# One attention burst a step, a second inverse on GpSimdE and the first network's weights on ScalarE's queue

## The chip, the cores and the metric

The kernel runs on one core of a Trainium2 chip. The metric is the device time of one execution in microseconds (us). TensorE does matmuls into the eight PSUM banks; VectorE, ScalarE and GpSimdE do the elementwise work (GpSimdE has no part in PSUM here); SyncE (SP) issues the DMAs. The engines run their own instruction lists in order and meet through semaphores.

## The reference

For 4 batches and 8 heads of 768 positions with 48 values a head, a delta rule carries a 48 x 48 state from position to position; its output, 3072 tokens of 384 values, goes through two networks (384 to 2048 to 384), the first with a rational function, the second with a squared relu:

```
for t in range(S):
    y[:, :, t] = q_t @ state
    v_old = state^T @ k_t                      # k_t normalised
    state = state + beta_t * outer(k_t, v_t - v_old)
h = x @ w_in; P = a0 + a1*h + a2*h**2 + a3*h**3; Q = 1 + |b0|*|h| + |b1|*h**2
x2 = (P / (Q + 1e-6)) @ w_out
h = x2 @ w2_in; r = max(h, 0); out = (r * r) @ w2_out
```

## The kernel before

**Attention.** The positions are cut into 12 chunks of 64, so there are 48 pieces (chunk, batch), each with all 8 heads, in 6 groups of 8. For each piece the 64 steps of the rule become matmuls with a 64 x 64 triangular inverse `T`. A group first needs its inverses: the products of the keys (`gram`, line 439) go through DRAM (`gs`) into `Gb`, a forward substitution fills `Tt`, and two matmul stages (`m1` line 619, `m2` line 633) join two 32 x 32 blocks to one of 64. Groups 0 and 1 substitute 15 steps of 16 x 16 blocks on VectorE (line 493) and join them with further 32 x 32 matmuls on TensorE (`ma`, `mb`, `mc`, lines 569 to 596) into 32 x 32 inverses. Groups 2 to 5 do 31 steps of 32 x 32 on GpSimdE (lines 502 to 508) and need no `ma`, `mb`, `mc`; the result goes through DRAM (`td`, `nd`). All groups use one `Gb`, one `Tt` and one `tmp`.

**One step.** A piece takes one step. `first` (line 729) makes `H` (keys times queries and state, `kv`) of piece k and, from group 1 on, `U` (`T` times the corrected values, `tv`) of piece k-1 beside it. `middle` (line 748) copies and masks `H` and corrects the values. `rest` (line 767) copies `U`, makes the output `Y` (`c3`, line 777) and then the state's increment `dS` (`ku`), with, in groups 1 to 3, the `gram` of piece n+16 beside it. `products` (line 711) interleaves generators two matmuls at a time; fp32 matmuls show up as two records each.

**PSUM.** Banks 0 to 2 accumulate the networks' second products (`acc`). Banks 3 to 5 are the pool `h`, for the first products; a bank of it is held from `mm1` until line 948 has read it for the last time. Banks 6 and 7 are the pool `att`; after group 0 attention has these two alone.

**The networks.** For each of 6 blocks of 512 tokens and each of 16 slices of the hidden layer there is a unit: `mm1` (line 912, 9 matmuls 128x512), the function (`rational`, line 931, eleven operations on ScalarE, VectorE and GpSimdE), `mm2_1` (line 953, 6 matmuls). The 96 units of the first network interleave with the attention of the groups to come; the second network's 96 units follow. A weight slice of 768 KB (fp64 bits) is loaded by SP (`dma`, line 330), turned into fp32 halves by ScalarE and VectorE (lines 863 to 870), and its remainder is made by GpSimdE (line 880). Ten of the 16 slices of the first network pass through two `raw` buffers.

**The order.** No order is written by hand. `Plan` lists every piece of work with an engine, an estimated duration, a due time and the tiles that it reads and writes; `play` simulates the engines greedily and the best of eight rounds is written out as each engine's list. Estimates and due times so set the order, and a wait is paid on the chip where an estimate is wrong. `PL.fill` adds matmuls on a constant where the plan sees TensorE idle near the start.

Of the kernel before, what the change touches and what calls it, by code (L numbers as in the profile page):

```python
# [19 lines left out]
C = 64  # L20
# [16 lines left out]
PREF = 1.5  # L37

# [204 lines left out]
def kernel(ctx, tc, kT, kS, qT, kn, vn, beta, par_in, w1, w2, outT):  # L243
# [55 lines left out]
    PL.fill = (T0 - 64, T0 + 20, lambda: nc.tensor.matmul(banks[2][:, 0:N // 2], ones[:, 0:128], ones, start=True, stop=True), 0.16, FILL)  # L299
# [6 lines left out]
    Gb, Tt = (x[:, 0:1024].rearrange("p (a b) -> p a b", b=32) for x in (Gbf, Ttf))  # L306
# [3 lines left out]
    tmp = at.tile([128, 256], F32, name="tmp")  # L310
# [14 lines left out]
    nd = [dram.tile([128, 32, 32] if g < 2 else [2, 32, 32, 32], F32, name=f"nd{g}") for g in range(NG)]  # L325
# [121 lines left out]
    def gstore(n, due):  # L447
        either(0.37, 0.36, lambda: (slot["Gs", n], ps(("G", n), [128, NP, C])), r=[("G", n)], w=[("Gs", n)], due=due,
            alloc=(("Gs",), ("Gs", n)), free=[("G", n)])
        dma(128, gs[n // 8][:, n % 8], lambda: slot["Gs", n], r=[("Gs", n)], w=[("gs", n)], due=due, free=[("Gs", n)])  # L450

    def attention(g):
        d0, d1 = inv_due(g)
        if g:
# [7 lines left out]
            for i in range(2):  # L462
                for j in range(2):
                    o = 64 * j + 32 * i
                    dma(128, Gb[o:o + 32], gv[j, i, :, :, 32 * i:32 * i + 32], lat=3.8, iss=0.6,
                        r=[("gs", 8 * g + ss) for ss in range(8)], w=[("Gb", o)], due=d0 - 3)
        else:
            add("DVE", 2.1, lambda: V.transpose(Gb, Dg.rearrange("r s p c -> r c (s p)")), lock=1,
                r=[("Dg", n) for n in range(8)] , w=[("Gb", o) for o in (0, 32, 64, 96)] + [("TT", 0)], due=d0)
        GB = [("Gb", o) for o in (0, 32, 64, 96)]  # L470
# [4 lines left out]
        add("POOL", 1.0, lambda: P_.memset(Tt, 0.0), w=["Tt"], due=d0)  # L475
# [13 lines left out]
        add("DVE", 0.25, lambda: V.tensor_copy(Tt.rearrange("p a b -> p (a b)")[:, 0:1024:33], nbr), r=["nbr"], w=["Tt"], due=d0, lock=1)  # L489
        for s in range(15 if g < 2 else 0):  # L490
# [7 lines left out]
            add("DVE", 0.42 + 4.0e-3 * a * b, st16, r=GB, w=["Tt", "tmp"], due=d1, lock=1)  # L498
        for s in range(31 if g > 1 else 0):
# [9 lines left out]
            for st in (st1, st2):  # L509
                add("POOL", 0.17 + 2.3e-3 * a * b, st, r=GB, w=["Tt", "tmp"], due=d1, lock=1)  # L510
# [5 lines left out]
        elif g == 1:  # L516
            for o in range(0, 128, 32):
                c0 = o % 64
                src = gs[g].rearrange("r s p c -> r (s p) c")[o + 16:o + 32, :, c0:c0 + 16]
                dma(32, Nb[o + 16:o + 32, :, :, 0:16].rearrange("r s p c -> r (s p) c"), src, lat=2.5, iss=0.6,  # L520
                    r=[("gs", 8 * g + ss) for ss in range(8)], w=[("N", o)], due=d1)


        if g:
            gv = gs[g].rearrange("r s p c -> r (s p) c")
            for o in (32, 96):
                if g == 1:
                    dma(128, TN[o:o + 32].rearrange("r s p c -> r (s p) c"), gv[o:o + 32, :, 0:32], lat=3.0, iss=0.6,
                        r=[("gs", 8 * g + ss) for ss in range(8)], w=[("TN", hf, o) for hf in range(2)], due=d1)
                for hf in range(2) if g > 1 else ():  # L530
# [3 lines left out]
        if g < 2:  # L534
            add("DVE", 2.0, lambda: V.transpose(Gb.rearrange("r q c -> r c q"), Tt.rearrange("p a b -> p b a")), r=["Tt"], w=GB, due=d1, lock=1)
            add("DVE", 2.0, lambda: V.transpose(DN.rearrange("r s p c -> r c (s p)"), Tt), r=["Tt"], w=["DN"], due=d1 + 1, lock=1)
        else:
            dma(512, td[g], Tt, r=["Tt"], w=[("td", g)], due=d1, lat=2.0)
            add("ACT", 2.05, lambda: A_.copy(Gb, Tt.rearrange("p a b -> p b a")), r=["Tt"], w=GB, due=d1)
# [10 lines left out]
        for i in (1, 0) if g > 1 else ():  # L550
            for j in range(2):
                o = 64 * j + 32 * i
                dma(128, TTv[o:o + 32, :, 32 * i:32 * i + 32], tdv[i, j], r=[("td", g)], w=[("TTx", g % 2, i, j)],
                    due=d1 + 2, lat=3.4, iss=0.6, after=[PL.last[wT[0]]] if wT[0] in PL.last else [])
        if g > 1:
            for j in range(2):
                dma(128, nd[g][j], Gb[64 * j:64 * j + 32], r=GB, w=[("nd", g, j)], due=d1 + 2)
                for hf in range(2):
                    x = 64 * j + 32 * hf
                    dma(64, TN[x:x + 32, 4 * hf:4 * hf + 4].rearrange("r s p c -> r (s p) c"), nd[g][j][16 * hf:16 * hf + 16].rearrange("q r c -> r q c"),  # L560
                        r=[("nd", g, j)], w=[("TN", hf, x)], due=d1 + 3, lat=3.2, iss=0.6)
                dma(64, TTv[64 * j:64 * j + 32, 16:32, 32:64], tdv[1, j][:, 16:32], r=[("td", g)], w=[("T", g % 2, 1, 64 * j)], due=d1 + 2, lat=3.2, iss=0.6)
# [3 lines left out]
        for hf in range(2 if g < 2 else 0):  # L566
# [47 lines left out]
        four = g > 1  # L614
        hs = range(2) if four else range(1)
        for hf in range(1 if four else 2):
# [33 lines left out]
            td_ = [("TD", g, hf, o) for o in range(0, 128, 32)] if g < 2 else []  # L650
# [78 lines left out]
        def first(k, k2, due):  # L729
# [374 lines left out]
```

## Time and profile before

| | |
|---|---|
| median of 3 runs | 1109.71 us (1107.1 to 1110.93) |
| the profiled execution | 1110.19 us, span of its instructions 1108.5 us |
| mean granted TensorE clock | 0.963 of 2.4 GHz |
| TensorE busy | 1057.7 us (95%) |
| VectorE, ScalarE, GpSimdE busy | 703.4, 647.6, 401.2 us |

The profiled execution lies 0.48 us above the median. Busy times are those of instructions in the profile; matmuls are pipelined, so their single durations overlap and a stretch is better measured from start to start.

### The profile page before, as it was taken

What the parts mean: (1) busy time and instruction counts of PE and PEld (TensorE: products, weight loads), DVE (VectorE), ACT (ScalarE), POOL (GpSimd) and SP (SyncE); (2) the same over time, 40 slices, a digit from 0 to 9 for tenths busy, and PEclk for the clock granted to TensorE, in tenths of its full rate; (3) what the DMA queues carried; (4) which work ended last, traced back from release to release, by engine and by line L of the source; (5) the groups of instructions that cost most, each with busy time, mean ns of one, the idle gap of its engine ahead of it and who ended that gap; (6) DMA issues with size and microseconds to landing.
All of it is one profiled execution on the core that took longest, in us unless ns stands there. A gap on an engine that the chain in (4) does not pass through costs nothing.

```text
span 1108.5 us, 24471 instructions
## 1 busy us (share of the span) xinstructions
PE 1057.7 (95%) x10014; PEld 752.1 (68%) x10014; DVE 703.4 (63%) x1124; ACT 647.6 (58%) x1173; POOL 401.2 (36%) x540
## 2 busy tenths in 40 slices
PE   6588999799989999999999899999999999999998
PEld 5576665466656666666666555688888888888887
DVE  5658889888658768766777599994334343333432
ACT  5264788676767777677778588754333242333422
POOL 6104589569628844972233143551000000000000
PEclk7677899999999999999999999999999999999999
DMA  7455326741650174034010220720001010000000
GB/s 235 120 144 166 75 90 190 166 128 31 144 116 34 50 161 110 5 103 83 29 28 12 90 85 30 252 89 29 29 0 57 1 51 8 1 29 1 29 1 29
DMA packets 120544, 84.01 MB, mean 76 GB/s; under 512 B 88048, under 2 KB 105584, under 8 KB 120432
## 3 DMA queue, kind: packets, MB, share of 16 engines
q1 hardware_dynamic: 120432, 82.44, 26.8%
q8 instruction: 79, 1.29, 0.5%
q14 instruction: 33, 0.27, 0.1%
HBM read 63.41 MB, written 17.83 MB: 73 GB/s over the span
## 4 chain that ended last, share of the span: by engine, by line
PE 84%; DVE 6%; POOL 3%; issue 3%; DMA 3%; ACT 1%; SPq 1%; DVEq 0%; ACTq 0%; POOLq 0%
PE bank L921 33%; PE bank L957 19%; PE bank L983 6%; PE bank L981 6%; PE bank L982 6%; PE bank L721 6%; PE bank L780 2%; PE bank L640 1%; POOL Tt L508 1%; DMA X<-in_qT_dram 1%; PE bank L626 1%; POOL tmp L504 1%; POOL mem L941 1%; PE bank L585 1%; DVE tmp L495 1%
## 5 line engine op out<-in xcount | busy, mean ns | idle before, releaser
L921 PE MATMUL bank<-xh,A 128*128 128x512 f32 x1152 | 360.6, 394 | 1.1 <-POOL A L880 1.1
L957 PE MATMUL bank<-mem,B 128*128 128x512 f32 x576 | 278.7, 615 | 0.7 <-DVE mem L948 0.7
L921 PE MATMUL bank<-xl,A 128*128 128x512 f32 x576 | 256.5, 445 | 6.0 <-DVE mem L948 5.2
L921 PEld LDWEIGHTS bank<-xh,A 128*128 128x128 f32 x1152 | 218.2, 190 | 63.4 <-issue 15.1
L941 POOL TENSOR_TENSOR mem<-mem 128x512 f32<-128x512 f32 x96 | 129.1, 1344 | 202.4 <-ACT mem L939 201.9
L957 PEld LDWEIGHTS bank<-mem,B 128*128 128x128 f32 x576 | 104.3, 192 | 97.5 <-issue 84.3
L969 DVE SCALAR_TENSOR_TENSOR mem<-bank,mem 128x512 f32<-128x512 f32 x96 | 66.3, 690 | 151.3 <-ACT mem L968 151.1
L968 ACT ACTIVATE mem<-bank 128x512 f32<-128x512 f32 x96 | 57.4, 598 | 152.9 <-PE bank L921 151.0
L921 PEld LDWEIGHTS bank<-xl,A 128*128 128x128 f32 x576 | 109.1, 189 | 45.9 <-issue 15.5
L983 PE MATMUL bank<-gh,C 128*128 128x512 f32 x288 | 113.7, 395 | 0.0
L981 PE MATMUL bank<-gl,C 128*128 128x512 f32 x288 | 113.5, 394 | 0.0
L982 PE MATMUL bank<-gh,C 128*128 128x512 f32 x288 | 112.0, 389 | 0.0
L972 DVE TENSOR_TENSOR gl<-mem,gh 128x512 fp32r<-128x512 f32 x96 | 71.5, 745 | 63.3 <-ACT gh L971 63.2
L946 DVE SCALAR_TENSOR_TENSOR mem<-mem,par,bank 128x512 f32<-128x512 f32 x96 | 71.3, 743 | 53.4 <-ACT bank L945 53.2
L971 ACT CAST gh<-mem 128x512 fp32r<-128x512 f32 x96 | 59.6, 621 | 74.8 <-DVE mem L969 62.0
L944 ACT ACTIVATE mem<-mem,par 128x512 f32<-128x512 f32 x96 | 69.3, 722 | 36.0 <-POOL mem L941 35.2
L942 DVE TENSOR_TENSOR mem<-bank,mem 128x512 f32<-128x512 f32 x96 | 65.8, 685 | 31.6 <-ACT mem L347 30.8
L938 ACT ACTIVATE mem<-bank 128x512 f32<-128x512 f32 x96 | 57.1, 595 | 46.1 <-PE bank L921 41.2
L939 ACT ACTIVATE mem<-mem,par 128x512 f32<-128x512 f32 x96 | 78.1, 814 | 2.3
L508 POOL TENSOR_TENSOR Tt<-Tt,tmp 128x31 f32<-128x31 f32 (+15 forms) x124 | 72.4, 584 | 8.2
L943 DVE SCALAR_TENSOR_TENSOR mem<-mem,par,bank 128x512 f32<-128x512 f32 x96 | 71.6, 745 | 3.9 <-ACT mem L938 1.4
L347 ACT COPY X<-bank 64x192 f32<-64x192 f32 (+1 forms) x184 | 62.0, 338 | 18.3 <-DVE vn L764 9.7
(124 smaller groups left out, 1546.4 us busy)
## 6 DMA issues: line engine op xcount, KB each, us to landing
raw<-in_w_dram SPq DMA_DIRECT2D x18, 768.0 KB, 5.5
B<-in_w_dram SPq DMA_DIRECT2D x10, 768.0 KB, 4.8
kTg<-in_kS_dram SPq DMA_DIRECT2D x40, 128.0 KB, 3.3
gs<-Gs SPq DMA_DIRECT2D x40, 128.0 KB, 2.5
kTc<-in_kT_dram SPq DMA_DIRECT2D x40, 128.0 KB, 2.5
X<-in_qT_dram SPq DMA_DIRECT2D x96, 48.0 KB, 2.9
kn<-in_kn_dram SPq DMA_DIRECT2D x12, 384.0 KB, 4.1
vn<-in_vn_dram SPq DMA_DIRECT2D x12, 384.0 KB, 3.6
```

The source lines that it names most:

```text
L508: P_.tensor_tensor(Tt[:, 0:a, s + 1:32], Tt[:, 0:a, s + 1:32], tv, op=ALU.subtract)
L921: M.matmul(h, a, b, start=(k == 0 and m == 0), stop=(k == NK - 1 and m == 2))
L939: add("ACT", 0.83, lambda: A_.activation(b(), a(), AF.Identity, bias=s(4), scale=s(5)), r=[ak, "par"], w=[bk], due=due + 3.3, alloc=(("b", ...
L941: add("POOL", 1.32, lambda: P_.tensor_tensor(b(), b(), a(), op=ALU.mult), r=[ak], w=[bk], due=due + 4.2, lock=1)
L943: add("DVE", 0.75, lambda: V.scalar_tensor_tensor(c(), c(), s(1), h(), op0=ALU.add, op1=ALU.mult), r=[hk, "par"], w=[ck], due=due + 6.3)
L944: add("ACT", 0.72, lambda: A_.activation(a(), b(), AF.Ln, bias=s(6)), r=[bk, "par6"], w=[ak], due=due + 6)
L946: add("DVE", 0.75, lambda: V.scalar_tensor_tensor(c(), c(), s(0), h(), op0=ALU.add, op1=ALU.mult), r=[hk, "par"], w=[ck], due=due + 8)
L957: M.matmul(acc[d], Bw[j][:, 128 * d:128 * d + 128], slot[gk], start=(j == 0), stop=(j == NJ - 1))
L972: add("DVE", 0.72, lambda: V.tensor_tensor(gl(), b(), gh(), op=ALU.subtract), r=[bk, gk, "late"], w=[lk], due=due + 5, lock=1, alloc=(("gl ...
L981: M.matmul(acc[d], wh, gl, start=(j == 0), stop=False)
L982: M.matmul(acc[d], wl, gh, start=False, stop=False)
L983: M.matmul(acc[d], wh, gh, start=False, stop=(j == NJ - 1))
```

## The change

Three things change together, and the plan makes a new order from all of them.

1. In groups 1 to 5 one `burst` a step takes the place of `first`, `c3` and `dS`: at step t it runs `c3` of piece t-2 and then, interleaved in one call of `products`, `kv` of piece t, `tv` of piece t-1, `ku` of piece t-2 and the `gram` of piece t-1+16. A group has 10 bursts. A burst allocates its banks together, up to three, from `att` and `h`; the `gram` lies in the rest of `U`'s bank. Copies between bursts are unchanged.
2. Group 1's inverse goes the way of groups 2 to 5: 31 steps on GpSimdE, `td` and `nd`, no `ma`, `mb`, `mc`, joined `m1` and `m2`. Even and odd groups have their own `Gb`, `Tt` and `tmp`. Its due times become 30 and T0 + 35. Latencies of `td`, `TTx`, `nd` and `TN` in the plan are raised.
3. The first network's 16 weight loads are issued by ScalarE, planned from 16 us on, 5.5 us apart; two tasks on the plan's pseudo engine LAND stand for their landing. The fill matmuls stop once `mm2_1` has begun. A scratch of the program for dynamic DMAs is cut to 1024 bytes.

```
-    tmp = at.tile([128, 256], F32, name="tmp")
+    tmps = [at.tile([128, 256], F32, name=f"tmp{i}") for i in range(2)]
...
         if g == 1:
-            return T0 - 10, T0 + 20
+            return 30, T0 + IV1
...
+        Gb, Tt, tmp = Gbs[q], Tts[q], tmps[q]
...
-        for s in range(15 if g < 2 else 0):
+        for s in range(0 if g else 15):
...
-        for s in range(31 if g > 1 else 0):
+        for s in range(31 if g else 0):
...
-        for hf in range(2 if g < 2 else 0):
+        for hf in range(0 if g else 2):
...
-        four = g > 1
+        four = g > 0
...
+        def burst(t, due):
+            r, w, al, fr, dur = [], [], [], [], 0.0
+            k0, k1, k2 = (x if 0 <= x < 8 else None for x in (t, t - 1, t - 2))
+            m = 8 * g + k1 + 16 if k1 is not None and g < NG - 2 else None
+            if k2 is not None:
...
+                w, al, dur = w + [("Y", n), ("dS", n)], al + [(("att", "h"), ("Y", n))], dur + 0.65
+            if k0 is not None:
...
+                w, al = w + [("H", n)], al + [(("att", "h"), ("H", n))]
+            if k1 is not None:
...
+                w, al = w + [("U", n)], al + [(("att", "h"), ("U", n))]
...
+            def go():
+                if k2 is not None:
+                    c3(8 * g + k2)
+                products(*([kv(k0)] if k0 is not None else []), *([tv(k1)] if k1 is not None else []),
+                         *([ku(k2)] if k2 is not None else []), *([gram(m, slot["U", m - 16][:, NP * D:NP * (D + C)].rearrange("r (p c) -> r p c", p=NP))] if m else []))
+            q = max((0.76 if k0 is not None else 0) + (0.36 if k2 is not None else 0), (0.37 if k1 is not None else 0) + (0.44 if m else 0))
+            add("PE", 0.22 + dur + q, go, r=r, w=w, due=due, alloc=al, free=fr)
...
+        for t in range(10 if g else 0):
+            dn = step_due(8 * g + t) if t < 8 else step_due(8 * g + 7) + 3 * (t - 7)
+            burst(t, dn)
+            if t < 8:
+                middle(t, dn + 1)
+            if 0 < t < 9:
+                ucopy(t - 1, dn + 1)
+            if t > 1:
+                result(t - 2, dn)
...
+        if l == 1:
+            add("ACT", 0.3, lambda: A_.dma_start(raw(rk), src[j]), w=[(rk, 0)], due=2 + 4.5 * j, alloc=None if e else (("raw",), rk), nb=WB + WS * j)
+            q = add("LAND", WS - 0.3, lambda: None, r=[(rk, 0)], w=["wq"], due=d0 - 4)
+            add("LAND", 2.5, lambda: None, w=[rk, (rk, 1)], due=d0 - 2, after=[q])
```

## Rows read from the trace of the kernel before

**Rows 1.** The page's first part: busy us (share of the span) xinstructions.
```profile
PE 1057.7 (95%) x10014; PEld 752.1 (68%) x10014; DVE 703.4 (63%) x1124; ACT 647.6 (58%) x1173; POOL 401.2 (36%) x540
```

**Rows 2.** Busy time of each engine in four stretches (granted clock, DMA share, GB/s last).
```profile
40.00:60.00 20.00, 13.23 (x623) 11.98 (x621) 6.70 (x10) 7.69 (x14) 2.43 (x2) 0.50 0.52 123
...
80.00:100.00 20.00, 15.37 (x524) 12.86 (x519) 18.69 (x30) 9.73 (x25) 11.90 (x12) 0.87 0.73 211
...
160.00:200.00 40.00, 38.74 (x510) 23.40 (x508) 36.98 (x59) 30.78 (x61) 37.38 (x52) 1.00 0.58 174
...
400.00:500.00 100.00, 99.44 (x1089) 61.54 (x1089) 73.04 (x125) 72.91 (x135) 63.52 (x97) 1.00 0.39 90
```

**Rows 3.** The chain that ended last, 340 to 400 us: start, us, what.
```profile
345.54 2.58 PE bank L957 x6
348.12 2.06 PE bank L921 x9
...
362.04 2.06 PE bank L921 x9
...
375.00 2.06 PE bank L921 x9
...
382.16 2.07 PE bank L921 x9
```

**Rows 4.** TensorE's timeline through one step with gram, 375 to 390 us.
```profile
377.00 0.26 PE L780 MATMUL bank<-X 112*48 112x64 f32 x1
...
377.58 0.25 PE L721 MATMUL bank<-X,kn 64*48 64x48 f32 x2
...
378.20 1.98 PE L957 MATMUL bank<-mem,B 128*128 128x512 f32 x4
380.12 0.31 PE L721 MATMUL bank<-X,kTc 48*64 48x112 f32 x2
...
381.03 1.13 PE L957 MATMUL bank<-mem,B 128*128 128x512 f32 x2
```

**Rows 5.** The same timeline in group 5, where no gram runs.
```profile
489.11 0.56 PE L721 MATMUL bank<-X,kn 64*48 64x48 f32 x16
489.61 0.50 PE L921 MATMUL bank<-xl,A 128*128 128x512 f32 x1
```

**Rows 6.** TensorE's timeline through the first network's first block.
```profile
103.50 0.80 PE L921 MATMUL bank<-xl,A 128*128 128x512 f32 x1
...
128.50 0.53 PE L585 MATMUL bank<-mem,DN 32*32 32x32 f32 x40 [1.76 <-issue]
...
201.36 0.67 PE L721 MATMUL bank<-vn,TT 64*64 64x48 f32 x16 [1.98 <-ACT X L347]
...
213.93 0.88 PE L921 MATMUL bank<-xh,A 128*128 128x512 f32 x2 [0.61 <-POOL A L880]
...
224.21 0.79 PE L921 MATMUL bank<-xl,A 128*128 128x512 f32 x1
```

**Rows 7.** VectorE's timeline before the first block: group 1's transposes.
```profile
82.33 2.07 DVE L535 STREAM_TRANSPOSE Gb<-Tt 128x1024 f32<-128x1024 f32 x1
...
87.52 1.95 DVE L536 STREAM_TRANSPOSE DN<-Tt 128x1024 f32<-128x1024 f32 x1
```

**Rows 8.** GpSimdE's substitutions of groups 2 to 5: busy us, mean ns.
```profile
L508 POOL TENSOR_TENSOR Tt<-Tt,tmp 128x31 f32<-128x31 f32 (+15 forms) x124 | 72.4, 584 | 8.2
...
L504 POOL TENSOR_TENSOR tmp<-Gb,Tt 128x31 f32<-128x31 f32 (+15 forms) x124 | 65.2, 526 | 9.7 <-DVE Tt L489 0.2
```

**Rows 9.** The tile raw up to 240 us: ns min/median/max.
```profile
L332 SPq DMA_DIRECT2D raw<-in_w_dram x12: 327/394/3859, 50.0 to 225.4; - x12
...
L865 DVE SCALAR_TENSOR_TENSOR raw<-raw x10: 959/1231/1978, 89.9 to 208.3; 128x768 uint32<-128x768 uint32 x10
```

**Rows 10.** What SP's queue waited for up to 200 us: us, times, longest.
```profile
SPq L332 <- POOL A L880: 11.6, 3, 5.2
```

**Rows 11.** The full timeline inside the step of rows 3, VectorE.
```profile
373.48 0.68 DVE L948 SCALAR_TENSOR_TENSOR mem<-bank,mem 128x512 f32<-128x512 f32 x1
```

More of the change, by code (lines that the diff above doesn't have):

```diff
@@ L298 @@
     nc.gpsimd.memset(ones, 1.0)
-    PL.fill = (T0 - 64, T0 + 20, lambda: nc.tensor.matmul(banks[2][:, 0:N // 2], ones[:, 0:128], ones, start=True, stop=True), 0.16, FILL)
+    begun = []
+    PL.fill = (T0 - 64, T0 + 20, lambda: begun or nc.tensor.matmul(banks[2][:, 0:N // 2], ones[:, 0:128], ones, start=True, stop=True), 0.16, FILL)
     X = [at.tile([128, 2, NP, 112], F32, name=f"X{b}") for b in range(B)]
@@ L324 @@
     td = [dram.tile([128, 32, 32], F32, name=f"td{g}") for g in range(NG)]
-    nd = [dram.tile([128, 32, 32] if g < 2 else [2, 32, 32, 32], F32, name=f"nd{g}") for g in range(NG)]
+    nd = [dram.tile([2, 32, 32, 32], F32, name=f"nd{g}") for g in range(NG)]
     y1 = [dram.tile([DM, N], F32, name=f"y1_{i}") for i in range(NT)]
@@ L526, in attention @@
             for o in (32, 96):
[L527 to L530, printed above, removed]
+                for hf in range(2):
                     x = o - 32 * hf
@@ L549, in attention @@
         wT = [("TT", g % 2)]
-        for i in (1, 0) if g > 1 else ():
+        for i in (1, 0) if g else ():
             for j in range(2):
@@ L553, in attention @@
                 dma(128, TTv[o:o + 32, :, 32 * i:32 * i + 32], tdv[i, j], r=[("td", g)], w=[("TTx", g % 2, i, j)],
-                    due=d1 + 2, lat=3.4, iss=0.6, after=[PL.last[wT[0]]] if wT[0] in PL.last else [])
-        if g > 1:
+                    due=d1 + 2, lat=4.5, iss=0.6, after=[PL.last[wT[0]]] if wT[0] in PL.last else [])
+        if g:
             for j in range(2):
-                dma(128, nd[g][j], Gb[64 * j:64 * j + 32], r=GB, w=[("nd", g, j)], due=d1 + 2)
+                dma(128, nd[g][j], Gb[64 * j:64 * j + 32], r=GB, w=[("nd", g, j)], due=d1 + 2, lat=4.2)
                 for hf in range(2):
@@ L649, in attention @@
             nd_ = [("TN", hf + h, o + 32 * h) for o in (0, 64) for h in hs]
-            td_ = [("TD", g, hf, o) for o in range(0, 128, 32)] if g < 2 else []
+            td_ = [("TD", g, hf, o) for o in range(0, 128, 32)] if g < 1 else []
             dup = [("T", g % 2, 1, o) for o in (0, 64)] if four else []
@@ L739, in first @@
                 r += [("T", g % 2, k2 // 4, o) for o in (0, 64)] + [("vn", n2 // B % 2, k2 % B)]
-                r += [("TD", g, k2 // 4, o) for o in range(0, 128, 32)] if g < 2 else []
+                r += [("TD", g, k2 // 4, o) for o in range(0, 128, 32)] if not g else []
                 r += [("TTx", g % 2, i, j) for i in range(2) for j in range(2)] + ([("TT", g % 2)] if g < 2 else [])
@@ L807, in rest @@
                         r=[("xin", c % 2, y) for y in range(B)], w=[("xin3", c % 2, j)], due=due + 7, iss=0.57)
+        def rest(k, due):
+            n = 8 * g + k
+            c, b = divmod(n, B)
+            yk, dk = ("Y", n), ("dS", n)
+            ucopy(k, due)
+            add("PE", 0.62, lambda: c3(n), r=cin(b), w=[yk], due=due + 2, alloc=(pl, yk))
+            add("PE", 0.55, lambda: products(ku(k)), r=[("Us", b, 0), ("Us", b, 1), ("kn", c % 2), yk], w=[dk], due=due + 3)
+            result(k, due)
@@ L809, in attention @@
         for k in range(8):
-            dn = step_due(8 * g + k)
             head(k)
-            if g:
-                first(k, k - 1 if k else None, dn)
-                middle(k, dn + 1)
-                if k:
-                    rest(k - 1, dn + 1)
-            else:
+            if not g:
+                dn = step_due(8 * g + k)
                 first(k, None, dn)
```

104 lines of the change are left out of this document (56 added, 48 removed).

## The prediction

> **What bounds the kernel now.** I read the page's busy times first: TensorE is busy 95% of the span, the next engine 63% [rows 1]. That is an average, so the second view is the busy time by stretch [rows 2]. Between 400 and 500 us TensorE is busy 99.44 of 100 at granted clock 1.00, its upper level of 2.4 GHz: there time is saved only by giving TensorE less to do. Between 40 and 60 us the clock is at the lower level, 1.2 GHz (0.50), and no engine is full; GpSimdE has 2.43 us of work in 20. From 80 to 100 VectorE is full (18.69 of 20), and from 160 to 200 GpSimdE is nearly so (37.38 of 40) beside a TensorE at 38.74. So there are three regimes: a start bound by latency, a crowded first block, and blocks bound by TensorE.
>
> The third view, the chain, prices a step of attention in the third regime. A unit without attention takes 2.58 for L957 and 2.06 for L921, 4.64 us; with a step in it the starts of L921 at 375.00 and 382.16 lie 7.16 apart [rows 3]. A step costs TensorE 2.52. The fourth view, TensorE's timeline, divides that [rows 4]: `c3` from 377.00 to 377.58, 0.58; `ku` with `gram` to 378.20, 0.62; `kv` with `tv` from 380.12 to 381.03, 0.91. These are 2.11. The other 0.41 are two changes between units and attention: four L957 at 0.43 (2.58 over 6) from 378.20 on would end at 379.92, and `kv` starts 0.20 later. Last, the first block [rows 6]: it starts at 103.50 and the seventeenth unit at 224.21, so 16 units take 120.7 us. Sixteen times 4.64 is 74.2, and group 1's attention is 8 x 2.52 and 0.7 for its last `tv`, 20.9. The other 25.6 go to group 1's merges, the next group's gram and joins, and waits.
>
> **The bursts.** `kv` and `ku` use the same two quarters of the array, by their rows and output partitions in the code, `tv` and `gram` the other two; so a burst lasts as long as `c3` and then `kv` and `ku` in turn, with `tv` and `gram` beside them. `ku` alone takes 489.11 to 489.61, 0.50 [rows 5]; of that I take 0.14 as start and end, which the burst already has in the 0.91. A full burst is 0.58 + 0.91 + 0.36 and one change of 0.20: 2.05 against 2.52, 0.47 less. Without `gram` a step before is 0.12 shorter (0.62 against 0.50), so 0.35 less. Of a group's ten bursts six are full. At the end `tv` of piece 7 goes beside `ku` of piece 6, which saves a change and most of that piece, 0.5. Groups 1 to 3 save 6 x 0.47 + 0.5 = 3.3 each, groups 4 and 5 6 x 0.35 + 0.5 = 2.6 each. For groups 2 to 5 that is 11.8; **I take -12**. Bounds: if in-order issue undoes the overlap, only one change is left, 6 x 0.20 + 0.2 = 1.4 a group, -6; if both changes and the end go, -17.
>
> The burst waits for the latest of its inputs and for three banks at once, and TensorE's next units stand behind it, then ScalarE's `Abs` of those units. A unit holds its bank from its `mm1` at 362.04 to the end of L948 at 373.48 + 0.68 = 374.16, 12.1 us [rows 3, 11]. If each bank of a burst is held twice the burst's 2.05, three are 12.3 us. Together 24.4 of the 5 x 6.69 = 33.5 bank-us of a new step: room, so I take 0, and the other end is a rival.
>
> **Group 1's inverse.** TensorE loses `ma`, `mb`, `mc` of one group and their stalls, VectorE 15 substitution pairs and two transposes of 2.07 and 1.95 us [rows 7]. GpSimdE gains 31 x (584 + 526 ns) = 34.4 us [rows 8]. It can start once group 1's products are back from DRAM, in the stretch where GpSimdE is idle 17.6 of 20 us [rows 2], and with the 11.90 us that GpSimdE has between 80 and 100 it ends between 80 and 105. Before, TensorE was still merging group 1 at 128.50, behind a stall of 1.76 [rows 6]. So group 1's steps can come some 20 us earlier. What that hits is the first block: late copies and weights at its end (1.98 and 0.61) and the merges. Those rows alone are 1.76 + 1.98 + 0.61 = 4.4; were all of the 25.6 to go but some 10 of the next group's gram and joins, 16. I take 11, nearer the middle, and with the burst's 3.3 **-14 for the first block**; bounds -3 (the bursts alone) and -19. **For the start I take -5**: 4.0 of transposes that stand among the full VectorE's last work ahead of 103.50, and 1 of merges. Bounds: +5, if GpSimdE's chain holds up the masks of group 0 (some nine waits behind an operation of about 0.55), and -10. Group 2's inverse, next on GpSimdE, has its own buffers and is not needed before the block's end.
>
> VectorE's L865 lasts 959 ns at least and 1978 at most [rows 9], so something holds it up at times. The Trainium skill (SBUF - State Buffer, the part on the shared port pair) states that a VectorE operation with two SBUF inputs and a GpSimdE operation that reads SBUF exclude each other for the whole instruction. The spread agrees with that, without naming the blocker; it speaks against this part of the change, and is a rival below.
>
> **The weights.** SP issues 16 loads fewer, at a median of 394 ns each [rows 9] 6.3 us, and for group 1 eleven DMAs more (17 in place of 6), 4.3: about even, and nothing waits for it, 0. The bytes are the same. ScalarE issues 16; its price for one isn't in the trace, so between 0 and SP's 6.3 us in all, and I take 6.3, hidden: ScalarE is busy 7.69 of 20 and 9.73 of 20 in the two early stretches [rows 2]. Without that cover it is at most 6.3 in the first block. Loads that wait for a `raw` buffer are another matter: SP waited 11.6 us in three waits for L880 [rows 10]. On ScalarE such a wait would hold PSUM copies, for which TensorE waits. The plan asks for loads from 16 us on, with VectorE and GpSimdE freer, so I take 0 and make 11.6 a rival. The Trainium skill (DMA: Bandwidth & Descriptors, Issuing engines are not separate DMA queues) states that all issuing engines share the same 16 DMA engines and that a second issuer saves only the issue time; no run here shows it yet, and by it the loads land no sooner, which is what the sum has. The scratch, the raised latencies and the end of the fill matmuls cost nothing by themselves: no DMA is issued by GpSimdE, and the others change the order only.
>
> **Sum.** 1110.2 (the profiled execution, 0.5 above the median) - 5 - 14 - 12 = **1079 us**.
>
> **Rivals.**
> - *Everything comes in full:* -10, -19, -17: 1064. For it: TensorE's waits ahead of the blocks. Against: some other engine is then next in the first block.
> - *GpSimdE and VectorE block each other:* 62 operations of 0.55 us among some 40 of VectorE's on eight weight slices. If two thirds of these wait 0.55, VectorE loses 15 us, all that it was relieved of: start 0, first block -9, bursts -12: 1089. The spread of L865 speaks for it, VectorE's idle time between 40 and 60 (13.3 of 20) against.
> - *Waits move to ScalarE's queue:* the 11.6 us of rows 10 come back in the first block and the start gains nothing: first block -3, bursts -12: 1095. For it: there are only two buffers as before. Against: the earlier loads.
> - *The change doesn't shorten TensorE's work:* in-order issue undoes the overlap, and the block's end waits for other engines: within 3 us of 1110. Against: 0.20 a change is in the rows.
> - *Slower:* the third bank. The estimate is 73% full, units come two at a time, and a unit that is late by one operation holds the burst and, behind it, all of TensorE. At 1 us a burst the 50 bursts cost 50: 1129. It decides from 32 / 50 = 0.64 us a burst on.
>
> **Chances and range.** The forecast, 1070 to 1087, 0.50; in full 0.12; VectorE and GpSimdE 0.10; ScalarE's queue 0.12; no change 0.06; slower 0.10. The likeliest gives 1079. The range leaves out the last two, 0.16, and reaches from a little under 1064, for bounds that all hold at once, to 1095 with 8 us for a bank wait of 0.16 us a burst: 1056 to 1103. Faster by over 0.3% (3 us, about what this kernel's measurements can tell from no change) is the first four, 0.84; within 0.3% 0.06; slower 0.10.
>
> **What would show it.** In the new profile: L921 starts in attention steps about 6.7 us apart, one stretch of L780, L781 and L721 a step; the first L921 near 98 and the seventeenth unit some 106 us later; GpSimdE busy from about 48 to 95 with L504 and L508; no `ma`, `mb` or `mc` (L574, L585, L596) after 65 us; ScalarE's queue with short waits. Wrong it would be with waits of TensorE's bursts for L948 (banks), bursts of 2.4 us or more, or ScalarE waiting at weight loads for L880.

## The result and the profile after

The changed kernel takes 1097.61 us (median of 4 runs, 1091.82 to 1097.83) against 1108.4 us, now the median of four runs of the kernel before: a ratio of 0.9885, 95% interval 0.9846 to 0.9924. The interval lies below 1, so the kernel is faster, by 1.2%; but of the 31 us forecast only 12.8 came (1110.2 to 1097.4, profiled executions).

In the new line numbers L966 is `mm1` (L921 before), L1003 `mm2_1`, L993 the last operation of a unit (L948), L925 the weights' low part on GpSimdE (L880), L779 and L780 `c3`, L720 the interleaved products, L625 and L639 the joins `m1` and `m2`, L512 and L516 the substitution.

The first view is the busy time by stretch, cut where a block of 16 units begins: the start, then blocks 1 to 5. First before, then after; after each duration come busy us and instructions of TensorE, its weight loads, VectorE, ScalarE, GpSimdE, then granted clock, DMA share, GB/s.

```profile
0.00:103.50 103.50, 75.17 (x2330) 65.10 (x2330) 67.02 (x141) 49.22 (x119) 34.24 (x62) 0.71 0.61 171
103.50:224.21 120.71, 112.67 (x1692) 72.45 (x1689) 102.89 (x161) 93.21 (x172) 85.02 (x110) 0.94 0.50 131
224.21:327.34 103.13, 99.69 (x1122) 61.52 (x1121) 78.03 (x130) 74.73 (x136) 65.49 (x95) 0.98 0.45 105
327.34:427.63 100.29, 99.61 (x1140) 61.80 (x1139) 71.93 (x122) 73.59 (x138) 63.59 (x97) 1.00 0.35 85
427.63:525.93 98.30, 97.07 (x1008) 60.40 (x1007) 71.85 (x121) 71.76 (x130) 62.58 (x96) 1.00 0.27 67
525.93:625.96 100.03, 99.83 (x766) 60.61 (x765) 70.42 (x116) 68.76 (x126) 26.91 (x32) 1.00 0.09 28
```

```profile
0.00:96.57 96.57, 69.10 (x1972) 61.40 (x1972) 61.33 (x117) 49.02 (x119) 59.22 (x100) 0.76 0.61 175
96.57:221.13 124.56, 105.51 (x1435) 69.32 (x1434) 99.65 (x165) 82.15 (x148) 102.02 (x136) 0.93 0.62 157
221.13:317.82 96.69, 96.64 (x1139) 61.67 (x1137) 78.64 (x135) 74.95 (x138) 64.91 (x95) 1.00 0.40 99
317.82:418.53 100.71, 96.54 (x1123) 61.99 (x1121) 69.28 (x121) 74.06 (x139) 61.73 (x96) 0.97 0.38 89
418.53:515.41 96.88, 95.53 (x1010) 60.84 (x1009) 70.90 (x118) 70.25 (x125) 61.55 (x96) 1.00 0.26 64
515.41:613.10 97.69, 97.58 (x767) 60.64 (x765) 69.07 (x115) 69.54 (x127) 26.89 (x32) 1.00 0.10 29
```

The start is 6.9 us shorter, the first block 3.9 longer, blocks 2 to 5 together 9.8 shorter (401.75 to 391.97); the rest is equal (482.5 and 482.6). In the first block TensorE's work did fall, by 7.2 us (112.67 to 105.51), but its idle time rose from 8.0 to 19.0. What it waited for there, after the change (us in total, times, longest):

```profile
PE bank L966 <- DVE mem L993: 7.5, 2, 5.8
PE bank L966 <- POOL A L925: 5.6, 2, 4.4
PE bank L779 <- ACT X L349: 1.9, 1, 1.9
PE bank L639 <- issue: 1.9, 1, 1.9
PE bank L720 <- ACT raw L908: 1.0, 1, 1.0
PE bank L720 <- DMA X<-in_qT_dram: 1.0, 1, 1.0
```

The longest is new. TensorE's and VectorE's timelines of the changed kernel show it:

```profile
123.75 0.79 PE L966 MATMUL bank<-xl,A 128*128 128x512 f32 x1 [5.76 <-DVE mem L993]
```

```profile
116.19 0.34 DVE L487 RECIPROCAL nbr<-nby 128x32 f32<-128x32 f32 x1
...
116.84 1.37 DVE L489 TENSOR_TENSOR nbr<-nbr,nby 128x32 f32<-128x32 f32 x1
118.25 1.18 DVE L490 TENSOR_SCALAR nrm<-nbr 128x32 f32<-128x32 f32 x1
...
120.30 1.22 DVE L496 TENSOR_TENSOR Gb<-Gb,nbr 128x1024 f32<-128x1024 f32 x1
...
123.00 0.69 DVE L993 SCALAR_TENSOR_TENSOR mem<-bank,mem 128x512 f32<-128x512 f32 x1
```

Group 2's normalisation (L487 to L497) stands in VectorE's queue ahead of a unit's last operations; the bank comes free only at L993. L487 starts without a wait, so it is the 5.5 us of these operations, from 116.19 to 121.66, that the unit stands behind, and 2.2 us of them are two operations that GpSimdE held up (see below).

The single burst looks as forecast. In the chain (start, us, what) one takes 0.58 for `c3` and 1.32 for the rest, and two lie 6.74 us apart (363.24, 369.98), where 7.16 were [rows 3]:

```profile
363.24 0.19 PE bank L779
...
363.82 1.32 PE bank L720 x41
365.14 2.26 PE bank L966 x9
367.40 2.57 PE bank L1003 x6
369.98 0.19 PE bank L779
```

### The profile page after: what moved, and what is told of

The parts are those of the page before. It is cut to its first block, busy times and chain, and to the rows that moved or that the text cites. A ratio compares the mean times of both kernels' runs of the same rounds, so it can differ in the third digit from the quotient of the medians.

```text
span 1095.7 us, 23222 instructions
## 1 busy us (share of the span) xinstructions
PE 1034.5 (94%) x9400; PEld 746.4 (68%) x9400; DVE 690.0 (63%) x1102; ACT 636.3 (58%) x1147; POOL 439.6 (40%) x602
## 4 chain that ended last, share of the span: by engine, by line
PE 79%; POOL 7%; DVE 6%; ACT 3%; issue 2%; DMA 1%; SPq 1%; POOLq 0%; DVEq 0%; ACTq 0%
PE bank L966 34%; PE bank L1003 18%; PE bank L1029 6%; PE bank L1027 6%; PE bank L1028 6%; PE bank L720 4%; POOL tmp L512 2%; PE bank L779 2%; POOL Tt L516 1%; POOL mem L986 1%; POOL X L758 1%; SPq L334 1%; PE bank L639 1%; ACT X L349 1%; PE bank L625 1%
## 5 line engine op out<-in xcount | busy, mean ns | idle before, releaser
L966 PE MATMUL bank<-xh,A 128*128 128x512 f32 x1152 | 362.6, 396 | 5.6 <-POOL A L925 5.6
L1003 PE MATMUL bank<-mem,B 128*128 128x512 f32 x576 | 272.1, 606 | 1.6 <-DVE mem L993 1.6
L966 PE MATMUL bank<-xl,A 128*128 128x512 f32 x576 | 256.0, 445 | 13.3 <-DVE mem L993 12.8
L966 PEld LDWEIGHTS bank<-xh,A 128*128 128x128 f32 x1152 | 219.9, 191 | 66.4 <-issue 13.1
L986 POOL TENSOR_TENSOR mem<-mem 128x512 f32<-128x512 f32 x96 | 127.8, 1331 | 175.5 <-ACT mem L984 175.1
L1003 PEld LDWEIGHTS bank<-mem,B 128*128 128x128 f32 x576 | 107.0, 192 | 99.2 <-issue 86.9
L966 PEld LDWEIGHTS bank<-xl,A 128*128 128x128 f32 x576 | 109.9, 191 | 59.0 <-DVE mem L993 17.4
L991 DVE SCALAR_TENSOR_TENSOR mem<-mem,par,bank 128x512 f32<-128x512 f32 x96 | 71.3, 742 | 46.4 <-ACT bank L990 46.1
L512 POOL TENSOR_TENSOR tmp<-Gb,Tt 128x31 f32<-128x31 f32 (+15 forms) x155 | 86.6, 558 | 28.8 <-DVE Tt L497 18.2
L516 POOL TENSOR_TENSOR Tt<-Tt,tmp 128x31 f32<-128x31 f32 (+15 forms) x155 | 92.9, 600 | 10.6
L349 ACT COPY X<-bank 64x256 f32<-64x256 f32 (+1 forms) x181 | 61.0, 339 | 29.6 <-DVE vn L763 11.9
```

What stands on the lines that cost most here:

```text
L349: A_.copy(a, b) if f is None else A_.mul(a, b, f) if g is None else A_.activation(a, b, AF.Identity, bias=f, scale=g)
L512: P_.tensor_tensor(tv, _mid(Gb[:, s, s + 1:32], [128, a, b]), Tt[:, 0:a, s:s + 1].to_broadcast([128, a, b]), op=ALU.mult)
L516: P_.tensor_tensor(Tt[:, 0:a, s + 1:32], Tt[:, 0:a, s + 1:32], tv, op=ALU.subtract)
L966: M.matmul(h, a, b, start=(k == 0 and m == 0), stop=(k == NK - 1 and m == 2))
L986: add("POOL", 1.32, lambda: P_.tensor_tensor(b(), b(), a(), op=ALU.mult), r=[ak], w=[bk], due=due + 4.2, lock=1)
L991: add("DVE", 0.75, lambda: V.scalar_tensor_tensor(c(), c(), s(0), h(), op0=ALU.add, op1=ALU.mult), r=[hk, "par"], w=[ck], due=due + 8)
```

## The experiments

All are the changed kernel with the edit named, unless said otherwise. The ratio is to the kernel before on the same chip, with its 95% interval; "first" and "second" are the first `mm1` of blocks 1 and 2, "idle" is the first block's length less TensorE's busy time, "third" the start of block 3; these four come from one profiled execution each. The code below is abridged; "..." stands for what is left out.

| run | median us | ratio | first | second | idle | third |
|---|---|---|---|---|---|---|
| before | 1108.4 | 1 | 103.5 | 224.2 | 8.0 | 327.3 |
| changed | 1097.6 | 0.9885 (0.9846-0.9924) | 96.6 | 221.1 | 19.0 | 317.8 |
| e1 inverse back | 1101.4 | 0.9931 (0.9907-0.9955) | 96.7 | 226.8 | 17.0 | 325.9 |
| e2 weights back | 1099.9 | 0.9912 (0.9890-0.9935) | 104.5 | 221.6 | 14.5 | 322.6 |
| e8 no bursts | 1104.1 | 0.9926 (0.9898-0.9954) | 96.9 | 221.9 | 14.3 | 321.2 |
| e20 bursts alone | 1102.4 | 0.9931 (0.9905-0.9957) | 104.3 | 224.1 | 7.3 | 327.1 |
| e3 half inverse | 1099.0 | 0.9899 (0.9873-0.9924) | 104.8 | 223.6 | 15.0 | 319.8 |
| e5 VectorE less | 1095.4 | 0.9850 (0.9828-0.9873) | 98.3 | 215.8 | 14.6 | 317.6 |
| e9 GpSimdE less | 1101.3 | 0.9905 (0.9885-0.9926) | 103.7 | 220.3 | 14.4 | 322.7 |
| e10 both less | 1096.8 | 0.9857 (0.9829-0.9885) | 110.0 | 220.5 | 7.7 | 320.9 |
| e4 second held | 1127.6 | 1.0155 (1.0131-1.0178) | 96.1 | 244.8 | 38.2 | 349.2 |
| e11 gram buffers | 1096.0 | 0.9861 (0.9828-0.9895) | 101.6 | 219.6 | 15.2 | 319.3 |
| e12 third raw | 1097.7 | 0.9885 (0.9856-0.9914) | 98.0 | 218.4 | 15.1 | 320.7 |
| e14 no reload | 1097.8 | 0.9884 (0.9858-0.9911) | 95.7 | 217.7 | 18.4 | 317.5 |
| e15 no norm 2 | 1095.6 | 0.9860 (0.9831-0.9888) | 96.8 | 218.9 | 15.2 | 317.6 |
| e16 stale products | 1096.2 | 0.9874 (0.9826-0.9922) | 95.5 | 216.0 | 16.1 | 314.6 |
| e13 more buffers | 1096.5 | 0.9877 (0.9844-0.9910) | 95.8 | 219.5 | 18.9 | 318.6 |
| e18 raw and scale | 1103.8 | 0.9945 (0.9924-0.9967) | 97.6 | 220.6 | 17.8 | 321.2 |
| e19 all relieved | 1095.7 | 0.9865 (0.9838-0.9892) | 107.7 | 213.8 | 5.5 | 316.0 |
| e21 loads moved | 1106.1 | 0.9961 (0.9945-0.9977) | 99.6 | 217.9 | 14.5 | 323.1 |

The profiled executions of e1 (1108.3 us) and e20 (1106.2) lie some 7 and 4 us above their medians, that of e16 (1092.2) 4 below. Each edit also lets the kernel's planner order the work anew; steps of 2 to 3 us in one column are therefore not read as the edit's doing.

**One part left out, or one alone.**

```diff
-        for s in range(0 if g else 15):      # e1
+        for s in range(15 if g < 2 else 0):
-            add("ACT", 0.3, lambda: A_.dma_start(raw(rk), src[j]), ...)      # e2
+        dma(768 ..., lambda: raw(rk), src[j], ...)
-        for t in range(10 if g else 0): ... burst(t, dn)      # e8
+            first(k, k - 1 if k else None, dn); middle(k, dn + 1); rest(k - 1, dn + 1)
```

> The changed kernel with group 1's inverse as in the kernel before (VectorE's substitution, the merges ma, mb, mc on TensorE); bursts, own buffers and ScalarE's weight loads stay. Theory A (the 34.4 us of group 1's inverse on GpSimdE, in one in-order queue with the masks and the units' products, are why the first block takes 124.6 us and not the forecast 106): the block falls to 120.7 - 3.3 for the bursts = about 117, the start loses its 4 us of transposes (first L966 near 100 in place of 96.6), and the time is about 1094. Theory C (the weight loads on ScalarE's queue lengthen the block) or theory D (the bursts do, since they wait for the latest of their inputs): the block stays at 122 to 126 and the time is 1098 to 1102.

> The changed kernel with the first network's weights asked for by SP's queue again, with the due times of the kernel before. Theory C: the block falls by some 5 us, the wait of 4.35 us for a weight slice at 204 us is gone, about 1092. Theory A: the block stays within 2 us of 124.6; the start may come later by the 2 to 3 us that earlier loads gave; 1097 to 1100.

> The changed kernel with the steps of the kernel before in place of the bursts, for groups 1 to 5 (two PSUM banks, two stretches of TensorE a step); group 1's inverse on GpSimdE and ScalarE's weight loads stay. If the bursts give what the forecast said, blocks 2 to 5 are 12 us longer together than with them and the second block starts 3 us later: 1110 to 1114. Theory D (bursts lengthen the first block by waiting for their latest input): the second block starts 3 us or more earlier than 221 us and the time is 1104 to 1108.

> The bursts alone: group 1's inverse as in the kernel before and the first network's weights on SP's queue again (the other buffers of the change stay). The forecast's steps give 15 us for the bursts in all, about 1095. From the runs that leave one part out, each part is worth 2 to 6 us and they add up to the 12.8 of the whole change: then the bursts alone give 4 to 6 us, 1104 to 1106.

(e20 has both edits of e1 and e2.) Theory A falls with e1: without the second inverse on GpSimdE the block is 130.1 us long, not 117, and even the 7 us by which that execution lies above its median would leave 123. Theory C's gain is not there either: with the weights back on SP's queue the block is 7.5 us shorter, but it begins 8.0 later, and the second block starts within 0.5 us of where it did. Theory D falls with e8 (221.9). So does what the forecast had for the bursts: without them blocks 2 to 5 are 6.2 us longer together, not 12. In e8 they are, in the columns of the first view:

```profile
221.93:321.23 99.30, 95.83 (x1116) 59.49 (x1115) 76.63 (x129) 74.44 (x137) 66.57 (x96) 1.00 0.39 98
321.23:421.98 100.75, 99.74 (x1141) 61.80 (x1139) 72.53 (x123) 73.22 (x136) 62.72 (x96) 1.00 0.36 85
421.98:520.19 98.21, 97.02 (x1008) 60.36 (x1007) 71.26 (x121) 72.49 (x132) 62.96 (x96) 1.00 0.27 67
520.19:620.10 99.91, 99.71 (x767) 60.60 (x765) 70.56 (x117) 68.77 (x126) 26.92 (x32) 1.00 0.09 28
```

Leaving a part out costs 0.46%, 0.27% and 0.41% of 1110 us: 5.1 for the inverse, 3.0 for the weights, 4.6 for the bursts, 12.7 together. The intervals of the four ratios overlap, so the order of the parts is not settled; bursts alone give 8 us (1110.4 to 1102.4), not the 4 to 6 expected in e20 and not the forecast's 15.

e20, e1, e2 and the changed kernel make a square of two parts, bursts present in all. Idle time of TensorE in the first block, from its first `mm1` to 130 us, from 130 to 170 and from 170 on:

| | merges on TensorE | inverse on GpSimdE |
|---|---|---|
| weights on SP | e20: 2.2 + 0.7 + 4.3 | e2: 6.2 + 0.9 + 7.4 |
| weights on ScalarE | e1: 3.9 + 2.0 + 11.1 | changed: 7.5 + 0.0 + 11.5 |

The move of the inverse takes 7.6 to 9.9 us of work from TensorE (113.1 to 105.5, 112.5 to 102.6) and gives 2.0 to 7.2 back as idle time in the block (17.0 to 19.0, 7.3 to 14.5), 3.6 to 4.0 of it up to 130 us. That the merges had filled time in which units wait is the likely reading; no run tries it by itself. The block gets 2.7 to 5.5 us shorter by the inverse. The earlier weights start the block 8 us sooner, bring 1.3 to 1.7 more idle before 130 us and 4 to 7 after 170, and make the block 7.5 to 10.3 us longer; the second block then starts between 0.5 us sooner and 2.8 later. The executions of e1 and e20 lie above their medians, so the ends of these ranges are rough.

**Which engine.** e3 drops `st2` for group 1, e5 the operation L910 for the first network, e9 the substitution loop for groups 1 and 2, e10 is e5 and e9.

```diff
-            for st in (st1, st2):      # e3
+            for st in (st1, st2) if g > 1 else (st1,):
-        for s in range(31 if g else 0):      # e9
+        for s in range(31 if g > 2 else 0):
```

> The changed kernel without the 31 subtractions of group 1's inverse: this leaves work out, so group 1's inverse is not computed. GpSimdE has some 16 us less to do ahead of group 1's bursts. Theory A: group 1's first full burst (c3, L779) comes 10 to 16 us earlier than at 147 us, TensorE's waits in the first block fall from 19 to about 10 us and the time to about 1088. Theories C and D: nothing hangs on when the inverse ends, the block stays at 122 to 126, 1096 to 1098.

> The changed kernel without one of VectorE's operations on each of the first network's 16 weight slices (L910, which puts the sign in; the weights come out without their sign). VectorE has some 19 us less to do before the second block, 10 of it in the first block; GpSimdE has as much as before. Theory F (VectorE's work, of which the change took nothing out of the first block: 102.9 us before, 99.7 after, sets its end): the second block starts at 210 to 214 in place of 221 us and the time is 1087 to 1091. Theory A' (GpSimdE's two inverses, masks and products set it): it starts at 219 to 223, 1096 to 1099.

> The changed kernel without the substitution steps of group 1's and group 2's inverses (L512, L516 of these groups: the two inverses are not computed). GpSimdE has some 69 us less to do before the second block, VectorE as much as before. Theory A': the second block starts 10 us or more earlier than 221 us, 1085 to 1089. Theory F: it starts at 217 to 223 us, and the time is 1093 to 1098.

> The changed kernel without both: VectorE's L910 on the first network's weight slices and the substitution steps of groups 1 and 2 (the weights have no sign, the two inverses are not computed). Theory F: as e5 or little better, second block at 208 to 214 us, 1085 to 1091. Theory G (the first block is full on several engines at once, so that the next one takes over as soon as one is relieved): clearly more than the two alone together, second block at 200 to 207 us, 1077 to 1084.

Taking the two inverses from GpSimdE (161.2 to 80.7 us of work before the second block) moves the second block's start by 0.8 us (e9), so theory A' falls. e3 and e9 show that the inverse's end doesn't date group 1's bursts either. In e3 the result leaves for DRAM at 92.6 us in place of 111.1, the join `m1` begins at 113.4 in place of 130.9, and the first `c3` of group 1 still comes at 148.1, as in the changed kernel; in e9, without any inverse to wait for, it comes at 151.2. Taking 19 us from VectorE brings 5.4 us (e5), less than the 7 to 11 of theory F. With both the block itself is 14 us shorter, 110.5, but begins 13 later. Around that beginning TensorE waited 8.8 us for gram loads (kTg) in e10, 10.8 in e9 and 10.7 in e3.

**Queues and buffers.**

```diff
-    tiles(at, "kTg", 2, ...); tiles(at, "Gs", 2, ...)      # e11
+    tiles(at, "kTg", 6, ...); tiles(at, "Gs", 4, ...)
+    PL.pools["raw"].append(one.tile([128, 2 * DM], w1.dtype, name="raw3"))      # e12
-            dma(512, td[g], Tt, ...)      # e14: these 17, for g == 2 nothing is issued
-                        ... w=[("Gb", q, o)], due=d0 - 3)      # e4
+                        ... w=[("Gb", q, o)], due=d0 - 3, nb=135 if g == 2 else 0)
```

> The changed kernel with six buffers in place of two for the loads of the gram (kTg) and four in place of two for its copies (Gs). Theory H (the chain load, gram, copy, store, load back of groups 1 and 2, through two buffers and SP's in-order queue, holds up the start and the normalisation of group 2, which stands in VectorE's queue): TensorE's waits of 10.4 us for kTg fall under 3 us, the wait of 5.8 us for L993 is gone, the second block starts at 212 to 216 in place of 221 us, 1088 to 1093. Otherwise the loads land no sooner, since the 16 DMA engines or something else are the limit: 219 to 223 us, 1095 to 1099.

> The changed kernel with a third buffer for weight slices (raw). Theory W (the last slices of the first block are late since each load waits for one of two buffers): TensorE's waits of 5.6 us for L925 are gone, the second block starts 4 to 5 us earlier, 1092 to 1094. Otherwise the gap is filled by another wait: 219 to 223 us, 1095 to 1099.

> The changed kernel without the DMAs that take group 2's inverse to DRAM and back (td, TT, nd, TN of this group: 17 DMAs in small packets on SP's queue, most of them between 193 and 215 us, where the 16 DMA engines are at a share of 1.0); its operands are stale. Theory S (SP's queue and the DMA engines in this stretch set when the second block starts): it starts at 210 to 214 in place of 221 us, 1086 to 1091. Otherwise, if the work of the compute engines sets it: 218 to 222 us, 1094 to 1098.

> The changed kernel with the loads of group 2's products into its inverse held back in the plan to 135 us, so that group 2's normalisation (VectorE) and inverse (GpSimdE) start some 15 to 20 us later. Theory A (GpSimdE's and VectorE's queues are crowded by two inverses at once): TensorE's wait of 5.8 us for L993 near 124 us is gone and masks wait less, the first block falls by 4 to 8 us, 1090 to 1094; should group 2's inverse then end too late, the second block takes back what the first gives, and the time is 1097 to 1102. Theories C and D: no change of the first block beyond 2 us.

e11 and e12 took away most of the wait that they were aimed at: L466 waits 1.9 us for kTg in e11, a unit 0.7 for L925 in e12. None of the first three moved the second block by more than 3.5 us; a unit's last operation (L993) still held TensorE for 7.2, 8.9 and 9.3 us. e4 was a miss of another kind: group 2's inverse, now late, stands in GpSimdE's queue ahead of a mask of group 1, and one burst waits 20 us for it. From TensorE's waits in e4's first block:

```profile
PE bank L779 <- POOL X L758: 20.1, 1, 20.1
```

**The wait for group 2's products.**

```diff
-        add("DVE", 2.2, r1, ...) ... add("DVE", 0.25, ... V.tensor_copy(Tt...)
+        if g != 2: (the same four)      # e15
-            gv = gs[g].rearrange(...)
+            gv = gs[1 if g == 2 else g].rearrange(...)      # e16, planned from 80 us on
```

> The changed kernel without group 2's normalisation on VectorE (L487 to L497 of this group; its inverse and scales are then stale). Theory V (group 2's normalisation stands in VectorE's in-order queue ahead of a unit's last operations, waits there for data that come back from DRAM at 114 to 124 us whatever is changed, and so stops TensorE at L993): the wait of 5.8 us for L993 near 124 us is gone, the sixth unit starts by 120 in place of 132 us and the second block at 213 to 216 in place of 221 us, 1090 to 1093. If the block is held by something else: second block at 218 to 222 us, 1095 to 1099.

> The changed kernel with group 2's inverse fed from group 1's products, which are in DRAM some 40 us earlier (group 2's inverse is then that of group 1's products); VectorE and GpSimdE do all of their work, and only the wait for group 2's gram, store and load is gone. Theory V: as without the normalisation, second block at 213 to 216 us, 1090 to 1093. If VectorE's and GpSimdE's work counts and not the wait: 218 to 222 us, 1095 to 1099.

The wait is gone in both (longest for L993: 1.6), and the sixth unit begins at 124 and 123 us in place of 132. Of these 8 us the second block's start keeps 2.2 and 5.1, the third's 0.2 and 3.2; e16's execution lies 4 us below its median. Theory V names a real wait, worth 2 to 5 us at the second block, not the cause of the whole; and in the changed kernel VectorE did not stand waiting for the products there, as the theory has it.

**All at once, and versions to beat it.** e19 has the edits of e9, e5, e16, e14 and e12; e13 those of e12 and four kTg buffers; e18 that of e12 and L496 on GpSimdE; e21 that of e12 and, from group 2 on, the loads of kn and vn on ScalarE's queue.

> The changed kernel with five of the single reliefs at once: without the substitution steps of groups 1's and 2's inverses (GpSimdE), without L910 on the first network's slices (VectorE), group 2's inverse fed from group 1's products, its 17 reload DMAs left out, and a third raw buffer (the two inverses are not computed, the weights have no sign). Theory G (the first block is held by several things in turn, each hidden just behind the next, so that no single relief pays): the reliefs together pay more than the 5 us that the best one did, second block by 208 us, the first block within 5 us of TensorE's own work of about 103 us. Rival: one thing that none of them touches (a fixed pace of units) holds the block: second block at 215 us or later.

> The changed kernel with a third buffer for weight slices and four buffers in place of two for the gram's loads, as a version that could beat it. If the two gains of the single edits add up (second block 1.5 and 2.7 us earlier): second block at 216 to 218 us and 1092 to 1095. If the next wait takes what each gives: 1095 to 1098.

> The changed kernel with a third buffer for weight slices and the 1024-wide scaling of the products (L496, 1.2 us on VectorE for each group) on GpSimdE from group 1 on, as a version that could beat it. Theory V: VectorE is held up 1.2 us less ahead of L993, second block at 216 to 219 us and 1092 to 1096; GpSimdE's queue gets some 2 us longer for each group and may take it back: 1096 to 1099.

> The changed kernel with a third raw buffer and with the loads of kn and vn from group 2 on asked for by ScalarE's queue, as a version that could beat it: in the third block TensorE loses some 4 us since vn lands late behind some 30 issues on SP's queue. If that is so, the third block falls from 100.7 to 97 us, 1092 to 1095. If ScalarE then waits for the buffers of kn and vn and holds PSUM copies, 1098 to 1105.

e19's busy time in the first block, in the columns of the first view, and below it the changed kernel's:

```profile
107.66:130.00 22.34, 17.70 (x236) 12.58 (x234) 15.81 (x27) 14.64 (x24) 6.03 (x6) 0.85 0.76 195
130.00:170.00 40.00, 40.00 (x519) 26.28 (x518) 34.59 (x61) 31.23 (x55) 16.07 (x18) 1.00 0.31 96
170.00:213.83 43.83, 42.98 (x704) 27.84 (x702) 38.64 (x68) 37.84 (x75) 18.61 (x18) 1.00 0.64 167
```

```profile
96.57:130.00 33.43, 25.92 (x117) 17.62 (x116) 23.91 (x37) 16.62 (x26) 26.82 (x45) 0.83 0.62 151
130.00:170.00 40.00, 40.00 (x707) 26.48 (x708) 36.78 (x61) 28.77 (x54) 37.96 (x48) 1.00 0.39 112
170.00:221.13 51.13, 39.59 (x625) 25.22 (x619) 38.95 (x68) 36.77 (x69) 37.24 (x45) 0.93 0.79 195
```

With five reliefs the block takes 106.2 us, the forecast's length, 5.5 of it idle, and after 130 us TensorE is idle for 0.9 us; none of the single ones came near (14.4 to 18.4 idle), and e10 with two had 7.7. That bears out theory G for the block after 130 us, and no fixed pace holds the units there. But its second half misses: the second block starts at 213.8 and not by 208, since the first `mm1` came 11 us later, after waits of TensorE for kTg (5.8) and for a copy (Gs, 4.2). None of the versions is measurably faster than the changed kernel: e13's interval overlaps its own, e21 is slower than it, and e18 is by its median. e21's third block took 104.3 us, not 97.

## Why the prediction was right and wrong

**The start, -5: measured -6.9 (96.57), but it is no gain, and the size is luck.** In the square it is the weights' doing, not the transposes': with the weights back it is 104.5 (e2), with the inverse back 96.7 (e1). The queue alone does not fix it: e3 and e9 keep the weights on ScalarE's queue and start at 104.8 and 103.7, behind TensorE's waits for kTg. And the second block starts at 221.6 without it and at 221.1 with it. The forecast took the first `mm1` for the end of the stretch bound by latency. That stretch reaches to 130 us: before the change TensorE had 24.7 us of work from its first `mm1` to 130 us, after it 25.9, in seven more microseconds.

**The first block, -14: measured +3.9. This is the step that failed, 18 us, as much as the whole miss.** Its 3.3 for the bursts were 0.5 to 0.9 (125.0 in e8 against 124.6; 120.7 before against 119.8 in e20). Its 11 for the inverse were 2.7 to 5.5 by the square. And the weights, which the sum had at nothing, lengthen the block by 7.5 to 10.3 us, since they move its beginning and not its end. The 11 rested on "ends between 80 and 105" and "group 1's steps can come some 20 us earlier". The inverse ran from 51.20 to 111 us, and cost 41.1 us of GpSimdE (L512 20.7, L516 20.4) in place of 34.4. Group 1's first `c3` did come sooner, but by 9.6 us, at 148.2 for 157.8 (the first start in each row, first before, then after):

```profile
L780 PE MATMUL bank<-X x64: 219/219/257, 157.8 to 205.4; 112*48 112x64 f32 x64
```

```profile
L779 PE MATMUL bank<-X x64: 218/219/258, 148.2 to 192.7; 112*48 112x64 f32 x64
```

An earlier end of the inverse, or none at all, moves it no further (148.1 in e3, 151.2 in e9): that the bursts' place in the plan's order among the units dates them is what is left, and was not tried by itself. So TensorE lost work and won waits: -7.2 and +11.0 in all. I had 25.6 us of merges, gram and waits in the block and took 11 off as if work taken from TensorE were time; it is that only where TensorE is never idle, from 130 to 170 us here.

**The bursts in blocks 2 to 5, -12: measured -9.8 for the whole change, 5 to 6 for the bursts.** The price of one burst was right: pitch 6.74 for 6.69, 1.90 and a change of 0.19 for a burst of 2.05 with its change. By blocks 6.4, -0.4, 1.4 and 2.3 against 3.3, 3.3, 2.6 and 2.6; the first of these holds 3.4 of idle time that block 2 had before. Against e8, which differs in the bursts alone, it is 6.2 (2.6, 0.0, 1.3 and 2.2 by blocks), and e20, which has the bursts alone, is 5.1 below the kernel before (401.75 to 396.64). So this term was about twice too large, and the 9.8 came near it by luck. The work did leave TensorE: in blocks 3 to 5 it is busy 6.8 us less than in e8 (296.5 to 289.7; forecast 8.5). But in the third block all of its 3.2 came back as idle time (1.0 in e8, 4.2 here). The third block lost some 4 us: GpSimdE's scaling of vn started at 403.92 after a wait of 10.62 for the load, and TensorE then waited 1.6 for L993 and 2.5 for L349. e12 and e13 have third blocks of 96.9 and 97.0, but second blocks of 102.3 and 99.1 for 96.7.

**Costed at nothing.** Banks: no burst waits for L993 in the first five blocks, so the third bank's rival fell. ScalarE's queue: ten loads at a median of 334 ns; ScalarE's waits for L925 up to the second block come to 2.0 us; that rival fell too. The Trainium skill (DMA: Bandwidth & Descriptors, Issuing engines are not separate DMA queues) has a second issuer save issue time only; by the landings the trace agrees (5.5 us at the median for ten loads from ScalarE's queue up to 221 us, 5.4 for the ten from SP's before), and still the start moved by 8 us; that SP's queue had stood waiting before [rows 10] is the likely reason, not one that was tried.

**VectorE and GpSimdE blocking each other**, the rival at 1089, was true in kind and small in size. GpSimdE paid with longer operations: the 62 of group 1's inverse took 41.1 us for 34.4, masks (L758) took 621 ns on average in the first block against 410 between 520 and 610 us, products (L986) 1447 against 1286: 3.8 and 2.6 us. VectorE paid less in these rows:

```profile
L909 DVE TENSOR_SCALAR raw<-raw 128x768 uint32<-128x768 uint32 x8 | 6.1, 760 | 0.0
L489 DVE TENSOR_TENSOR nbr<-nbr,nby 128x32 f32<-128x32 f32 x2 | 1.6, 782 | 0.1
```

```profile
L909 DVE TENSOR_SCALAR raw<-raw 128x768 uint32<-128x768 uint32 x8 | 4.5, 558 | 0.1
L489 DVE TENSOR_TENSOR nbr<-nbr,nby 128x32 f32<-128x32 f32 x2 | 0.4, 194 | 0.1
```

The upper rows are the changed kernel's groups by line between 97 and 221 us, the lower ones e9's, without the two inverses: 2.8 us. L865 had raised the suspicion [rows 9], but its mean (now L910) is 1266 ns with the inverses and 1268 without. What held up VectorE in group 2's normalisation is on GpSimdE's timeline of the changed kernel:

```profile
116.70 1.47 POOL L675 TENSOR_TENSOR vn<-vn,nT 128x768 f32<-128x768 f32 x1
118.13 1.26 POOL L986 TENSOR_TENSOR mem<-mem 128x512 f32<-128x512 f32 x1
```

L489 (1.37 us, 194 ns on average in e9) ends at 118.21, 0.04 us after L675, and L490 (1.18 us, 182 ns in e9) at 119.43, 0.04 after L986: 2.2 us of the 5.5 ahead of L993. The Trainium skill (SBUF - State Buffer, SBUF: two separate sides) has the loser wait for the whole instruction; L489 at 1.37 us fits that. The blockers here are the scaling of vn and a unit's product, not the inverse. So leaving the inverses out doesn't end it: in e9 it is L497 that takes 1.28 us, from 127.39 on, beside an L986 from 127.36 to 128.62.

**Open.** Why an earlier end of the first block is mostly given back in the second: e5 won 5.4 us and lost 5.2 again, there with a wait of 3.2 us for the copy between `m1` and `m2`, e19 with one of 3.5 for L999 (its L993). The third block starts between 314.6 and 323.1 us in all runs but e1, e4 and e20. That the planner's order sets this is argued, not tried.

## What to carry to other kernels

Work taken from the busiest engine is time only in stretches where that engine is never idle; elsewhere ask what it was filling, and expect waits to return for a part of it (here 2.0 to 7.2 of idle for 7.6 to 9.9 of work). A change of several parts should be priced by leaving each one out: a sum that looks right for a stretch (9.8 for 12) can hide a part that gave half. The end of a start-up is not the first instruction of the main loop but the point from which the bound engine runs without gaps; what comes sooner than that is not won. Where one relief after the other yields nothing, take several away at once before looking for yet another single cause.

## What the runs showed of the hardware

The two waits of over 4 us in the first block cost TensorE more than their length. After the 5.76 us ahead of 123.75 the next unit's nine L966 took 4.21 us, against 2.26 with a change ahead of them in the chain shown above; the granted clock from 123.75 to 127.95 was 0.50, the lower of its two levels (1.2 and 2.4 GHz, 0.5 and 1.0), and from 110 to 120 us 1.00. After the 4.35 us for L925 that ended at 204.56 the granted clock was 0.59 up to 212.06, and six L1003 took 3.99 us, 2.73 where the clock was 1.00 (at 115.26). The chain of the changed kernel, and TensorE's timeline behind the second wait:

```profile
123.75 4.21 PE bank L966 x9
127.95 3.03 PE bank L1003 x6
```

```profile
208.14 3.99 PE L1003 MATMUL bank<-mem,B 128*128 128x512 f32 x6
```
